# The matmuls of probabilities and values of a group, kept together and with the second head first

## The chip, the cores and the metric

The kernel runs on one core of a Trainium2 chip. The core has a matrix engine (TensorE, called PE; its weight loads are listed apart as PEld), VectorE (DVE), ScalarE (ACT), GpSimd (POOL) and SyncE (SP), which here issues the DMAs. Each engine works through its own queue in order and waits on semaphores for the others. TensorE writes to PSUM, in banks of 512 fp32 columns. The metric is the time of one execution on the device, in microseconds.

## The reference

Causal attention with a forget gate, over 4 batches, 8 heads, 576 positions and 64 values per head, and after it two feed-forward layers on the 2304 tokens:

```python
scores = scale * np.matmul(q, k.transpose(0, 1, 3, 2))
log_f = np.log(np.clip(f, 0.0001, 1.0))
cum = np.cumsum(log_f, axis=-1)
decay = cum[:, :, :, None] - cum[:, :, None, :]
scores = np.where(causal, -1000000000.0, scores + decay)
attn = np.exp(scores - np.max(scores, axis=-1, keepdims=True))
attn = attn / (np.sum(attn, axis=-1, keepdims=True) + 1e-09)
x = np.matmul(attn, v)                                  # then heads side by side: 2304 x 512
x = np.maximum(np.maximum(x @ w1, x @ w2), x @ w3) @ w_out          # d_ff 768
h = x @ w_in                                                        # d_ff 2048
P = a[0] + a[1] * h + a[2] * h*h + a[3] * h*h*h
Q = 1.0 + np.abs(b[0]) * np.abs(h) + np.abs(b[1]) * h*h
out = (P / (Q + 1e-06)) @ w_out2
```

## The kernel before, in words

Attention goes by pairs of heads, 20 pairs in all: the first batch has four pairs for the queries 0 to 319 (group 0) and again four for the queries 320 to 575 (group 1); each later batch has four pairs that do both groups. A unit is one head of a pair in one group; its names end in pair, head, group (`tp0_16_1_1` is of pair 16, head 1, group 1).

A unit goes through three steps of the outer loop (line 536). In its first step `scores` computes q times k into PSUM (L343, L345, L346), VectorE takes mask and row minimum (L347), ScalarE the exponential (L353), and `normalise` lets GpSimd scale the rows (L362). In the next step `turn` transposes the probabilities on TensorE, bank by bank (L382), and ScalarE copies them into `pt` (L384), which holds both heads of a group side by side. In the third step `attend` multiplies them with the values (L397), for both heads at once: it does nothing for head 0 and does the whole group when head 1 comes.

A group in `attend` has one PSUM bank `o`. Head 0 goes into partitions 0 to 63 and head 1 into 64 to 127 (`SIDES`). So each matmul has 64 columns of weights (the values of one head in one chunk of 128 keys), and the probabilities stream through. Group 0 has three key chunks, of 320, 256 and 128 queries; group 1 has five, four of 256 queries and one of 128. The program's order is chunk by chunk, and in each chunk head 0 and then head 1. These matmuls are plain fp32, and the trace has two records for each. A copy on ScalarE (L402) and a subtraction on VectorE (L403) then take the bank into the tile `x`, the input of the first feed-forward layer.

Between these pieces the loop puts, at six points of every step (`fill`), matmuls of the first feed-forward layer of finished batches: `moe1_h` (L427 to L429, tiles `h`) and `moe1_o` (L452 to L454, tiles `x2p`), and conversions of weights that are still to come. During the first four pairs, when there is no such work, `exercised` starts two matmuls without use (L84) ahead of each bank.

The engines' queues do not follow the program's order. All instructions up to line 762 are laid out by a scheduler with a timeline of its own: of the instructions whose inputs it takes as ready it picks by priority, normally the place in the program. `keep_in_program_order` (called by `pinned`, line 227) adds an edge from an instruction to the one traced just before it on the same engine, so that the two are not swapped; `tc.high_priority()` lets what is traced inside go first among the ready ones. After the attention comes the rest of the first layer with the conversion of the next weights (`raw_wi`, `convert_wi`), and then the second feed-forward layer, with an order written out by hand (line 763).

Of the kernel before, what the change touches and what calls it, by code (L numbers as in the profile page):

```python
# [37 lines left out]
def kernel(  # L38
    ctx: ExitStack, tc: tile.TileContext, q, k, v, f, w1, w2, w3, w_out, m2_in, m2_out, m2_a, m2_b, out
):  # L40
    nc = tc.nc
# [11 lines left out]
    def r32(ap):  # L53
        return ap.bitcast(F32)
# [25 lines left out]
    def exercised(bank, n):  # L80

        if n < 4:
            for _ in range(WARM):
                nc.tensor.matmul(bank, warm[:, 0], wide, start=True, stop=True)  # L84
        return bank
# [57 lines left out]
    for g in range(2):  # L143
        pts.append(apool.tile([P, 2, GCOLS[g]], F32, name=f"pt{g}", tag=f"pt{g}"))
        col = GCH[g][0][0]
# [81 lines left out]
    def pinned(ld):  # L227
        tc.keep_in_program_order(ld)
# [10 lines left out]
    SIDES = [(slice(0, D), slice(D, P)), (slice(D, P), slice(0, D))]  # L239
# [73 lines left out]
    class Unit:  # L313
# [72 lines left out]
        def attend(self):  # L386

            p, h, g = self.pair, self.h, self.g
            if h == 0:
                return  # L390
            lo, hi = GQ[g]
            w = hi - lo
            ot = exercised(ps_o.tile([P, 512], F32, name=f"o_{self.nm}", tag="o"), p.n)
            order = list(GCH[g].items())
            for j, (c, (col, q0)) in enumerate(order):
                for i in range(2):
                    nc.tensor.matmul(  # L397
                        ot[SIDES[i][0], q0 - lo : w], p.v[:, c, i], p.pt[g][:, i, col : col + hi - q0],
                        start=(j == 0), stop=(j == len(order) - 1),
                    )  # L400
            x = mpool.tile([P, 2, w], F32R, name=f"x_{self.nm}", tag=f"x{g}", bufs=(6, 8)[g])
            nc.scalar.activation(x[:, 0], ot[:, :w], AF.Copy)  # L402
            nc.vector.tensor_tensor(x[:, 1], ot[:, :w], r32(x[:, 0]), op=ALU.subtract)  # L403
            xt[p.b, p.hp, g] = x
# [390 lines left out]
```

## Time and profile before

| What | us |
| --- | --- |
| median of three timed runs | 983.41 (982.66 to 983.57) |
| span of the profiled execution, first to last instruction | 980.7 |
| PE busy, PEld busy | 962.0, 836.0 |
| VectorE, ScalarE, GpSimd busy | 742.8, 628.5, 254.1 |
| L397, matmuls of probabilities and values, 512 records | 78.5 |

The profiled execution has no time of its own beside its span; the 2.7 us between the span and the median lie before the first and behind the last instruction. Busy time of PE is the union of its records. Matmuls are pipelined, so records overlap: the time that one takes from the queue is read from its start to the next start, and not from its own length. L397 ends at about 496.5 us.

### The profile page before, as it was taken

To read this page: it belongs to the slowest core of one execution; us is meant where nothing else is said; L and a number is where in the kernel's file an instruction comes from. 1 tells how busy PE (TensorE), PEld (TensorE's weight loads), DVE (VectorE), ACT (ScalarE), POOL (GpSimd) and SP (SyncE) were. 2 spreads that over 40 slices of the span, in tenths; PEclk is the share of its full clock that TensorE was granted. 3 is DMA by queue.
4 is the path that set the end of the run, shared out by engine and by line. 5 is a ranking of instruction groups with operands and counts; after the bars stand their busy time and mean duration, and the time that the engine had idled before them with its cause. 6 is when DMAs were issued, how large, how long until landed. Compare 5 with 4: busy or idle time off the path is not lost.

```text
span 980.7 us, 16825 instructions
## 1 busy us (share of the span) xinstructions
PE 962.0 (98%) x5780; PEld 836.0 (85%) x5780; DVE 742.8 (76%) x1756; ACT 628.5 (64%) x1457; POOL 254.1 (26%) x408
## 2 busy tenths in 40 slices
PE   8989999999999999999999999999999999999998
PEld 6757898887889888999899987888888888899997
DVE  5789985556676777535367949988988888899997
ACT  5776666667666666646444538766666766677775
POOL 2555664445454545424223310000000000000000
PEclk9989999999999999999999999999999999999999
DMA  6594232124446455220054659011002100200000
GB/s 162 153 250 135 76 86 70 42 64 116 133 132 185 122 150 162 76 73 24 8 155 146 199 170 345 1 43 43 1 1 65 44 0 24 84 1 1 33 1 33
DMA packets 125621, 88.52 MB, mean 90 GB/s; under 512 B 74448, under 2 KB 110304, under 8 KB 125536
## 3 DMA queue, kind: packets, MB, share of 16 engines
q1 hardware_dynamic: 125536, 87.45, 29.8%
q8 instruction: 46, 0.75, 0.3%
q14 instruction: 39, 0.32, 0.1%
HBM read 64.73 MB, written 22.69 MB: 89 GB/s over the span
## 4 chain that ended last, share of the span: by engine, by line
PE 77%; DVE 6%; DMA 1%; issue 1%; ACT 1%; SPq 1%; POOL 0%; DVEq 0%; ACTq 0%
PE oo L718 7%; PE oo L719 7%; PE oo L717 7%; PE hq L668 6%; PE hq L670 6%; PE hq L669 6%; PE o L397 6%; PE h L427 5%; PE h L429 5%; PE h L428 5%; PE tp L382 4%; PE s L345 2%; PE s L346 2%; PE x2p L452 2%; PE x2p L454 2%; PE x2p L453 2%
## 5 line engine op out<-in xcount | busy, mean ns | idle before, releaser
L427 PE MATMUL h<-x,w1h 128*128 128x320 f32 (+1 forms) x576 | 177.1, 308 | 3.4 <-DVE m L434 3.0
L428 PE MATMUL h<-x,w1h 128*128 128x320 f32 (+1 forms) x576 | 172.3, 299 | 0.0
L429 PE MATMUL h<-x,w1l 128*128 128x320 f32 (+1 forms) x576 | 172.1, 299 | 0.0
L427 PEld LDWEIGHTS h<-x,w1h 128*128 128x128 f32 x576 | 109.6, 190 | 11.4 <-DVE m L434 5.2
L353 ACT ACTIVATE e<-e,st 128x64 f32<-128x64 f32 (+4 forms) x160 | 89.4, 559 | 46.0 <-DVE st L347 43.9
L362 POOL TENSOR_SCALAR e<-e,rs 128x64 f32<-128x64 f32 (+4 forms) x160 | 90.2, 578 | 105.5 <-DVE rs L359 80.9
L718 PE MATMUL oo<-wp,gh 128*128 128x512 f32 x288 | 112.8, 392 | 0.0
L717 PE MATMUL oo<-wp,gh 128*128 128x512 f32 x288 | 112.4, 390 | 0.0
L428 PEld LDWEIGHTS h<-x,w1h 128*128 128x128 f32 x576 | 109.8, 191 | 0.7 <-issue 0.6
L429 PEld LDWEIGHTS h<-x,w1l 128*128 128x128 f32 x576 | 109.6, 190 | 0.6 <-issue 0.6
L719 PE MATMUL oo<-wp,gl 128*128 128x512 f32 x288 | 108.8, 392 | 0.0
L677 ACT ACTIVATE s<-hq 128x512 f32<-128x512 f32 (+1 forms) x80 | 44.3, 554 | 96.9 <-PE hq L670 96.7
L347 DVE CUSTOM_DVE_ANT_0 e<-s,mask 128x320 f32<-128x320 f32 (+3 forms) x160 | 67.8, 433 | 49.2 <-PE s L346 34.6
L384 ACT ACTIVATE pt<-tp 128x384 f32<-128x384 f32 (+3 forms) x160 | 69.1, 470 | 19.6 <-PE tp L382 16.5
L680 DVE SCALAR_TENSOR_TENSOR s<-s,ab,u 128x512 f32<-128x512 f32 (+1 forms) x80 | 55.8, 698 | 31.3 <-ACT u L678 31.1
L382 PE MATMUL tp<-ident,e 128*128 128x128 f32 (+1 forms) x480 | 77.7, 282 | 0.9 <-POOL e L362 0.9
L397 PE MATMUL o<-pt,v 128*64 128x256 f32 (+2 forms) x512 | 78.5, 369 | 0.0
L670 PE MATMUL hq<-x,wil 128*128 128x512 f32 (+1 forms) x192 | 70.4, 366 | 0.0
L668 PE MATMUL hq<-x,wih 128*128 128x512 f32 (+1 forms) x192 | 70.4, 366 | 0.0
L669 PE MATMUL hq<-x,wih 128*128 128x512 f32 (+1 forms) x192 | 70.3, 366 | 0.0
L719 PEld LDWEIGHTS oo<-wp,gl 128*128 128x128 f32 x288 | 54.1, 188 | 11.7
L717 PEld LDWEIGHTS oo<-wp,gh 128*128 128x128 f32 x288 | 54.1, 188 | 11.0
(129 smaller groups left out, 2434.6 us busy)
## 6 DMA issues: line engine op xcount, KB each, us to landing
raw_w<-in_moe_w_dram SPq DMA_DIRECT2D x18, 512.0 KB
raw_wp<-in_moe_w_out_dram SPq DMA_DIRECT2D x32, 256.0 KB
wpd<-wp SPq DMA_DIRECT2D x32, 256.0 KB
raw_wi<-in_moe_w_in_dram SPq DMA_DIRECT2D x32, 256.0 KB
wp<-wpd SPq DMA_DIRECT2D x10, 768.0 KB
x2d<-xo SPq DMA_DIRECT2D x16, 320.0 KB
out_dram<-ob SPq DMA_DIRECT2D x18, 256.0 KB
kn<-in_k_dram SPq DMA_DIRECT2D x32, 128.0 KB
```

Source lines behind the costliest of these rows:

```text
L362: nc.gpsimd.tensor_scalar(e, e, self.rs[:, 1, j : j + 1], 0.0, op0=ALU.mult, op1=ALU.add)
L382: nc.tensor.transpose(tp[:kr, dst : dst + P], self.e[i][:, Q0[c] : Q1[c]], ident)
L397: nc.tensor.matmul(ot[SIDES[i][0], q0 - lo : w], p.v[:, c, i], p.pt[g][:, i, col : col + hi - q0], start=(j == 0), stop=(j == len(order) - 1),
L427: nc.tensor.matmul(hp_[:, :w], wh[:, j, dc], xs[dc][:, 1], start=(dc == NDC - 1), stop=False)
L428: nc.tensor.matmul(hp_[:, :w], wh[:, j, dc], xs[dc][:, 0], start=False, stop=False)
L429: nc.tensor.matmul(hp_[:, :w], wl[:, j, dc], xs[dc][:, 0], start=False, stop=(dc == 0))
L668: nc.tensor.matmul(hp_[:, :w], wih[:, dc, fs], xh, start=(dc == 0), stop=False)
L669: nc.tensor.matmul(hp_[:, :w], wih[:, dc, fs], xl, start=False, stop=False)
L670: nc.tensor.matmul(hp_[:, :w], wil[:, dc, fs], xh, start=False, stop=(dc == NDC - 1))
L717: nc.tensor.matmul(o, g[0][:, ts_], wh_, start=(fc == 0), stop=False)
L718: nc.tensor.matmul(o, g[0][:, ts_], wl_, start=False, stop=False)
L719: nc.tensor.matmul(o, g[1][:, ts_], wh_, start=False, stop=(fc == NF2 - 1))
```

## The change

In `attend` the loop over heads runs second head first. All matmuls of the group are traced at high priority, and each but the first is pinned to the one before it. The matmuls themselves, their operands and their bank are the same; the last `stop` of each half stays at the last chunk. Three lines are added, so that every line behind 400 has a number higher by three (L397 becomes L398, L427 becomes L430).

```diff
--- before.py
+++ after.py
@@ -392,12 +392,15 @@
             w = hi - lo
             ot = exercised(ps_o.tile([P, 512], F32, name=f"o_{self.nm}", tag="o"), p.n)
             order = list(GCH[g].items())
-            for j, (c, (col, q0)) in enumerate(order):
-                for i in range(2):
-                    nc.tensor.matmul(
-                        ot[SIDES[i][0], q0 - lo : w], p.v[:, c, i], p.pt[g][:, i, col : col + hi - q0],
-                        start=(j == 0), stop=(j == len(order) - 1),
-                    )
+            with tc.high_priority():
+                for j, (c, (col, q0)) in enumerate(order):
+                    for i in (1, 0):
+                        mm = nc.tensor.matmul(
+                            ot[SIDES[i][0], q0 - lo : w], p.v[:, c, i], p.pt[g][:, i, col : col + hi - q0],
+                            start=(j == 0), stop=(j == len(order) - 1),
+                        )
+                        if (j, i) != (0, 1):
+                            pinned(mm)
             x = mpool.tile([P, 2, w], F32R, name=f"x_{self.nm}", tag=f"x{g}", bufs=(6, 8)[g])
             nc.scalar.activation(x[:, 0], ot[:, :w], AF.Copy)
             nc.vector.tensor_tensor(x[:, 1], ot[:, :w], r32(x[:, 0]), op=ALU.subtract)
```

The queue of PE, group 1 of pair 16, before. Tiles `h` are the first feed-forward layer, `tp` transposes of probabilities, `s` scores. First the place at which the first matmul of the group stands:

```order
L427 MATMUL h1_2_0_3_5552<-x_12_1_0_3448,w1h_3_751 128x320
L428 MATMUL h1_2_0_3_5552<-x_12_1_0_3448,w1h_3_751 128x320
L429 MATMUL h1_2_0_3_5552<-x_12_1_0_3448,w1l_3_752 128x320
L397 MATMUL o_16_1_1_5572<-pt1_124,v_16_5029 64x256
L382 MATMUL tp0_16_1_1_5474<-ident_82,e3_16_1_1_5423 128x128
L382 MATMUL tp1_16_1_1_5498<-ident_82,e3_16_1_1_5423 128x128
L382 MATMUL tp2_16_1_1_5503<-ident_82,e3_16_1_1_5423 64x128
L345 MATMUL s0_0_17_1_0_5627<-k1s3_1339,q1s01_1627 128x64
```

and then, 44 rows further on, the place of the other nine:

```order
L382 MATMUL tp1_17_0_0_5619<-ident_82,e1_17_0_0_5515 64x128
L382 MATMUL tp1_17_0_0_5619<-ident_82,e2_17_0_0_5546 64x128
L429 MATMUL h0_2_0_4_5644<-x_12_1_0_3448,w1l_4_853 128x320
L397 MATMUL o_16_1_1_5572<-pt1_124,v_16_5029 64x256 x7
L397 MATMUL o_16_1_1_5572<-pt1_124,v_16_5029 64x128 x2
L427 MATMUL h1_2_0_4_5664<-x_15_1_0_4896,w1h_4_852 128x320
L428 MATMUL h1_2_0_4_5664<-x_15_1_0_4896,w1h_4_852 128x320
```

The same group after:

```order
L431 MATMUL h0_2_0_4_5644<-x_13_1_0_3914,w1h_4_852 128x320
L382 MATMUL tp0_17_0_0_5586<-ident_82,e1_17_0_0_5515 128x128
L382 MATMUL tp0_17_0_0_5586<-ident_82,e2_17_0_0_5546 128x128 x2
L382 MATMUL tp1_17_0_0_5619<-ident_82,e0_17_0_0_5509 64x128
L382 MATMUL tp1_17_0_0_5619<-ident_82,e1_17_0_0_5515 64x128
L398 MATMUL o_16_1_1_5572<-pt1_124,v_16_5029 64x256 x8
L398 MATMUL o_16_1_1_5572<-pt1_124,v_16_5029 64x128 x2
L382 MATMUL tp1_17_0_0_5619<-ident_82,e2_17_0_0_5546 64x128
L345 MATMUL s2_0_17_1_0_5639<-k1s3_1339,q1s01_1627 128x320
```

The lone matmul has joined the other nine, and they stand as one block: eight of 256 queries and two of 128.

In front of that block, after: the last transposes of the second head, from which its probabilities are copied. 28 rows stand between the last of them and the block, 20 of them `h`:

```order
L382 MATMUL tp0_16_1_1_5474<-ident_82,e4_16_1_1_5429 128x128
L382 MATMUL tp0_16_1_1_5474<-ident_82,e3_16_1_1_5423 128x128
L382 MATMUL tp0_16_1_1_5474<-ident_82,e4_16_1_1_5429 128x128
L382 MATMUL tp1_16_1_1_5498<-ident_82,e4_16_1_1_5429 128x128 x2
L382 MATMUL tp2_16_1_1_5503<-ident_82,e4_16_1_1_5429 64x128
L345 MATMUL s0_0_17_1_0_5627<-k1s3_1339,q1s01_1627 128x64
L430 MATMUL h2_2_0_3_5601<-x_15_1_0_4896,w1h_3_751 128x320
L431 MATMUL h2_2_0_3_5601<-x_15_1_0_4896,w1h_3_751 128x320
L432 MATMUL h2_2_0_3_5601<-x_15_1_0_4896,w1l_3_752 128x320
```

Before, 28 rows stood there too, in front of the nine matmuls, with a somewhat different mix.

The second place is early, group 1 of pair 4, the first group behind which first-layer work is there to fill. Before, seven matmuls stand behind the first two `h` tiles, and the other three further on:

```order
L429 MATMUL h1_0_0_0_911<-x_1_1_0_516,w1l_0_227 128x320
L427 MATMUL h1_0_0_0_911<-x_0_1_0_369,w1h_0_226 128x320
L428 MATMUL h1_0_0_0_911<-x_0_1_0_369,w1h_0_226 128x320
L429 MATMUL h1_0_0_0_911<-x_0_1_0_369,w1l_0_227 128x320
L397 MATMUL o_4_1_1_1028<-pt1_124,v_4_738 64x256 x7
L427 MATMUL h2_0_0_0_971<-x_3_1_0_841,w1h_0_226 128x320
L428 MATMUL h2_0_0_0_971<-x_3_1_0_841,w1h_0_226 128x320
```

After, all ten stand ahead of the first `h` tile, directly behind the transposes of pair 4 and one score matmul:

```order
L382 MATMUL tp1_4_1_1_962<-ident_82,e4_4_1_1_903 128x128 x2
L382 MATMUL tp2_4_1_1_967<-ident_82,e4_4_1_1_903 64x128
L343 MATMUL s4_1_5_1_1_1129<-kf3_113,qf3_117 128x256
L398 MATMUL o_4_1_1_1028<-pt1_124,v_4_738 64x256 x8
L398 MATMUL o_4_1_1_1028<-pt1_124,v_4_738 64x128 x2
L430 MATMUL h0_0_0_0_862<-x_3_1_0_841,w1h_0_226 128x320
L431 MATMUL h0_0_0_0_862<-x_3_1_0_841,w1h_0_226 128x320
L432 MATMUL h0_0_0_0_862<-x_3_1_0_841,w1l_0_227 128x320
L430 MATMUL h0_0_0_0_862<-x_2_1_0_661,w1h_0_226 128x320
```

Over the whole queue the 32 groups stand in 65 pieces before and in 32 after.

## Rows read from the trace of the kernel before

**Rows 1.** the page: span, busy time of the engines, chain that ended last

```profile
span 980.7 us, 16825 instructions
PE 962.0 (98%) x5780; PEld 836.0 (85%) x5780; DVE 742.8 (76%) x1756; ACT 628.5 (64%) x1457; POOL 254.1 (26%) x408
PE 77%; DVE 6%; DMA 1%; issue 1%; ACT 1%; SPq 1%; POOL 0%; DVEq 0%; ACTq 0%
```

**Rows 2.** windows: length, busy us (instructions) by engine, clock, DMA share, GB/s

```profile
0.00:62.00 62.00, 57.16 (x296) 42.85 (x297) 41.10 (x128) 43.26 (x118) 22.91 (x41) 1.00 0.67 181
62.00:120.00 58.00, 52.18 (x297) 43.09 (x296) 56.81 (x119) 36.40 (x85) 36.31 (x38) 0.85 0.45 127
120.00:500.00 380.00, 377.19 (x2809) 338.21 (x2809) 229.48 (x773) 236.00 (x671) 167.91 (x297) 1.00 0.35 98
500.00:981.00 481.00, 475.49 (x2383) 411.82 (x2381) 415.41 (x739) 312.85 (x585) 26.99 (x32) 1.00 0.20 68
```

**Rows 3.** PE's groups from 119 to 500 us: busy, mean ns, idle before

```profile
L345 PE MATMUL s<-k1s,q1s 128*128 128x448 f32 (+1 forms) x150 | 47.1, 321 | 1.3 <-DVE q1s L287 1.0 <-DVE st L347 0.4
L452 PE MATMUL x2p<-hh,wo 128*128 128x320 f32 (+1 forms) x144 | 43.9, 307 | 1.3 <-DVE xo L457 1.3
```

**Rows 4.** the chain around the last block of L397: start, us, what

```profile
494.40 2.10 PE o L397 x17
496.82 3.59 DMA raw_wi<-in_moe_w_in_dram
```

**Rows 5.** timeline of PE (start, us): rest of a split group, a whole group

```profile
27.08 1.40 PE L397 MATMUL o<-pt,v 128*64 128x320 f32 x10
...
351.56 1.41 PE L397 MATMUL o<-pt,v 128*64 128x320 f32 x12
```

**Rows 6.** timeline of PE: a lone matmul (two records) over 256 columns

```profile
92.32 0.31 PE L428 MATMUL h<-x,w1h 128*128 128x320 f32 x1
92.47 0.31 PE L429 MATMUL h<-x,w1l 128*128 128x320 f32 x1
92.71 0.65 PE L397 MATMUL o<-pt,v 128*64 128x256 f32 x2
93.28 0.41 PE L427 MATMUL h<-x,w1h 128*128 128x320 f32 x1
93.53 0.30 PE L428 MATMUL h<-x,w1h 128*128 128x320 f32 x1
```

**Rows 7.** timeline of PE: a lone matmul over 320 columns

```profile
57.60 0.75 PE L397 MATMUL o<-pt,v 128*64 128x320 f32 x2
58.28 0.48 PE L343 MATMUL s<-kf,qf 66*128 66x256 f32 x1
```

**Rows 8.** timeline of PE: the rest of a split group of ten

```profile
405.56 2.16 PE L397 MATMUL o<-pt,v 128*64 128x256 f32 x18
```

**Rows 9.** timeline: last transposes and last copy of that group's second head

```profile
400.86 0.82 PE L382 MATMUL tp<-ident,e 128*128 128x128 f32 x6
...
402.56 0.37 ACT L384 ACTIVATE pt<-tp 64x256 f32<-64x256 f32 x1
```

**Rows 10.** low clock: a wait of PE, a window, two h matmuls in it

```profile
65.09 0.90 PE L382 MATMUL tp<-ident,e 128*128 128x128 f32 x3 [0.65 <-POOL e L362]
...
66.00:78.00 12.00, 9.83 (x31) 7.16 (x32) 11.90 (x27) 8.06 (x18) 8.76 (x9) 0.50 0.55 158
...
77.17 0.47 PE L427 MATMUL h<-x,w1h 128*128 128x320 f32 x1
77.44 0.47 PE L428 MATMUL h<-x,w1h 128*128 128x320 f32 x1
```

**Rows 11.** windows of L397 alone: length, PE, PEld, clock, DMA, GB/s

```profile
20.00:62.00 42.00, 8.62 (x48) 4.33 (x48) 1.00 0.76 211
62.00:120.00 58.00, 6.24 (x42) 3.23 (x42) 0.85 0.45 127
120.00:500.00 380.00, 63.68 (x423) 33.00 (x422) 1.00 0.35 98
```

## Prediction

> **What bounds the kernel now.** I read the page's busy shares and its chain first, then a table of windows by stage, then TensorE's waits, and last the changed line, L397, piece by piece in the timeline. The span is 980.7 us; with the 2.7 us that lie around it in the timed runs this is the median of 983.4 us, and I work every sum against that. PE is named busy for 98% of the span and holds 77% of the chain that ended last [rows 1]. By stage [rows 2]: up to 62 us the pipeline fills; from 62 to 120 us VectorE is busy 56.8 of 58 us and PE runs partly at a low granted clock; from 120 to 500 us PE is busy 377 of 380 us while VectorE and ScalarE are at about 60%; after 500 us the last feed-forward work runs, without any L397. In the long stretch PE waits for almost nothing: 1.3 us before the scores and 1.3 us before x2p are its only waits of a microsecond or more [rows 3]. So between 120 and 500 us the time is the sum of what PE has to start, one matmul after the other, and anything taken out of that queue comes off the end.
>
> What follows 500 us moves along rather than absorbing it: the chain goes from the last block of L397 at 494.40 straight to the first load of raw_wi at 496.82 [rows 4], and the conversions that fill the next stage hang on that load.
>
> **The change, part by part.** L397 writes two heads into two halves of one bank: each matmul uses 64 of the 128 columns of the array. Two such matmuls of different heads run side by side. The one whole group in the trace shows it: its six matmuls last 1.41 us, and the rest of a split group, with one matmul less, lasts 1.40 us [rows 5]. The first matmul of the first head, when it stands next to its partner, is free.
>
> Before, it mostly does not stand there. The first head's probabilities are ready a step earlier, so the scheduler put its first matmul alone into some other work, and the remaining nine or five matmuls later. A group of the first kind is 320 queries by three key chunks (six matmuls), one of the second 256 queries by five (ten). In the order, the 32 groups are in 65 pieces: 14 groups of the first kind have their first matmul apart, and so have 15 of the second, whose 16th (pair 4) is broken further in; three of the first kind have a break (or one more) before the last chunk; only one stands whole. After, the 32 groups are 32 pieces, all with heads alternating.
>
> What a lone matmul costs, over 256 columns [rows 6]: it starts at 92.71 and the next starts at 93.28, so 0.57 us. The matmul in front of it takes 0.24 us to the next start instead of the 0.15 us of its neighbour: 0.09 us. The one behind takes 0.25 us instead of 0.15: 0.10 us. Sum 0.76 us. Over 320 columns [rows 7]: 0.68 us from start to start, and with the same 0.19 us of entry and exit 0.87 us.
>
> What the rest costs does not grow when the lone one returns: for the first kind of group it is seen (1.40 against 1.41 us). For the second kind no whole group is in the trace. The rest of a split one lasts 2.16 us for 18 records [rows 8]; the second head has all five of its chunks in there and the first head only four, so the second head's column half sets the length and the fifth chunk lies beside it. Bounds: 2.16 us if that holds, 2.16 + 0.57 us if not. I take 2.16, since the smaller group behaves so.
>
> The sum of PE time removed: 16 groups of the second kind x 0.76 = 12.2 us; 14 of the first kind x 0.87 = 12.2 us; three further breaks at 0.2 us (entry and exit alone) = 0.6 us. Together 25.0 us. By stage: four lone matmuls before 62 us, 3.5 us; two groups between 62 and 120 us, 1.5 us; the rest, 20.0 us, in the stretch where PE is the bound.
>
> Of the 5.0 us before 120 us I take half, 2.5 us: the bounds are 0 (VectorE, 56.8 of 58 us busy, sets the pace there [rows 2]) and 5.0 (up to 62 us PE is busy for 57.2 us [rows 2], and VectorE's work would start earlier too).
>
> **What the change adds** is one wait per group: the whole block now stands behind the second head's copy of the probabilities, and PE issues in order, so all behind it would stand too: the transposes of the next unit, whose copies ScalarE would get late, and the h matmuls. In the trace, for the group of pair 16, the last transposes start at 400.86 and end at 401.68, and the last copy starts at 402.56 and takes 0.37 us, so it lands at 402.93; the block starts at 405.56 [rows 8, 9]. The copy needs 1.3 us behind the transposes. In the new order 28 rows stand between these transposes and the block: 20 h matmuls at 0.15 us [rows 6], four score matmuls and five transposes, about 3.8 us (an estimate from these durations). Ahead of nearly all blocks the new order keeps such a distance, a little shorter than before; only pair 4's block stands close behind its transposes, in the stretch that PE does not bound. So I price new waits at the size of the existing ones: 0 at best, 2.6 us (a doubling of the two waits of [rows 3]) at worst, taken at 1.3 us. Bringing the rest of the program into another order costs nothing by itself: the count of h, score and transpose matmuls is the same, and a change between transposes and full matmuls is paid before and after alike.
>
> ScalarE, VectorE, GpSimd and the queues get the same instructions. Their loads move by a few places only, and the DMA share of 0.35 from 120 to 500 us leaves room for all of it to come 5% sooner [rows 2].
>
> Forecast: 983.4 - 20.0 - 2.5 + 1.3 = 962.2, so **962 us**. Its own range: with all 25.0 us and no new wait 958.4, with the two present waits gone too 955.8; with nothing gained before 120 us and all new waits 966; I let it reach 969.
>
> **Rivals.** [...]
>
> *PE is not the bound, and the time goes into waits.* Weight loads fill 338.2 of the 380 us only [rows 2], so 41.8 us are left, more than the 20 us removed; were those waits in disguise, the block would merely wait longer elsewhere and the time stay at 983. Against it: L397 itself holds the weight loads for only 33.0 of its 63.7 us [rows 11], which explains 30.7 of the 41.8. [...]
>
> *Slower: the copy is late at every block.* If PE reached each block when the second head's last transposes are just done, it would stand for the 1.3 us worked out from [rows 9] at each of 32 blocks, 41 us, against 25 us removed: 983 + 16 = 999. It decides where less than about 0.5 us of other PE work stands between (1.3 less the 0.8 us that a group gains). The order has this at one block of 32.
>
> *The heads do not pair as written,* since each chunk now starts with the second head. Then only entry and exit are saved, 33 x 0.19 = 6 us: 977. The 1.41 us of the whole group [rows 5] speak against: alternation is what pairs, and which head leads should not matter.
>
> **How the numbers follow.** Forecast 0.74 (956 to 969); early stretch or new waits eat a part 0.11 (969 to 979), the pairing rival with it 0.03; better than computed 0.03; no change 0.04; slower 0.05. The range 955 to 976 holds the first and about half of the second. A measurement of this kernel tells about 0.2%, 2 us, from no change: faster 0.91, within 0.04, slower 0.05.
>
> **What would show it.** In the new trace the attention line should be in 32 pieces of 1.41 and 2.16 us, 57 us busy in sum against 78.5 now [rows 11]; the last block should start near 473 us against 494.40 [rows 4]; the time from there to the end should be as now. PE's waits should not show a new one of more than 1 us on ScalarE's copy in front of the block. I would be wrong if the last block starts less than 12 us earlier, if a whole group of the second kind lasts over 2.3 us, or if the part after the last block is longer than before.

## The result: 15 us faster, and the profile after

| | before | after |
| --- | --- | --- |
| median of the timed runs, us | 983.49 (982.66 to 983.73) | 968.42 (966.44 to 970.9, 4 runs) |
| span of the profiled execution, us | 980.7 | 969.1 |

The ratio is 0.9849, with a 95% interval of 0.9837 to 0.9861: 15 us faster. The prediction was 962 us, in a range of 955 to 976. The profiled execution of the changed kernel took 970.9 us, the longest of its four, so the two traces are only 11.6 us apart. On record each execution takes 1.8 us more than its span (970.9 against 969.1); the 2.7 us that I put around the span before hold, beside these, 0.9 us by which that execution was shorter than the median. I work sums against the traces and keep verdicts to the medians.

The page after, answering to [rows 1], and the table of cores, whose last number is the mean granted clock:

```profile
span 969.1 us, 16846 instructions
...
PE 943.1 (97%) x5780; PEld 829.9 (86%) x5780; DVE 739.6 (76%) x1756; ACT 623.8 (64%) x1457; POOL 252.4 (26%) x408
...
PE 70%; DVE 14%; DMA 6%; ACT 4%; issue 3%; POOL 2%; SPq 1%; ACTq 0%; POOLq 0%; DVEq 0%
```

```profile
core 0: 969.1 us, clock 0.988
```

PE's busy time fell by 18.9 us, from 962.0 to 943.1, but the span by 11.6 only. What is not busy rose from 18.7 (980.7 less 962.0) to 26.0 us. VectorE now holds 14% of the chain that ended last, where it held 6%. The windows, answering to [rows 2]:

```profile
0.00:62.00 62.00, 54.79 (x300) 41.42 (x300) 41.24 (x134) 44.15 (x122) 23.87 (x42) 1.00 0.69 183
62.00:120.00 58.00, 51.61 (x299) 42.80 (x299) 54.13 (x113) 35.36 (x86) 37.28 (x40) 0.85 0.43 123
120.00:500.00 380.00, 373.72 (x2890) 346.32 (x2889) 240.89 (x805) 239.10 (x684) 169.90 (x301) 0.99 0.37 103
...
120.00:160.00 40.00, 37.59 (x255) 34.06 (x254) 27.29 (x87) 24.75 (x69) 17.80 (x31) 0.91 0.34 93
160.00:485.00 325.00, 321.13 (x2531) 297.27 (x2530) 200.21 (x683) 206.82 (x596) 147.58 (x264) 1.00 0.37 103
```

Up to 62 us PE does 2.4 us less than in [rows 2] in the same 62 us: the work was taken out, and PE stood still instead. From 120 to 160 us it is idle for 2.4 us, at a clock of 0.91. From 160 us on it is nearly full again. PE's timeline shows the blocks, answering to [rows 5, 8] (the last row is the last block of all, answering to [rows 4]):

```profile
341.17 0.28 PE L430 MATMUL h<-x,w1h 128*128 128x256 f32 x1
341.38 1.41 PE L398 MATMUL o<-pt,v 128*64 128x320 f32 x12
342.72 0.39 PE L431 MATMUL h<-x,w1h 128*128 128x256 f32 x1
...
396.27 2.17 PE L398 MATMUL o<-pt,v 128*64 128x256 f32 x20
...
481.35 2.17 PE L398 MATMUL o<-pt,v 128*64 128x256 f32 x20
```

They are as forecast: 12 records in 1.41 us, 20 in 2.17 us, 32 pieces. From start to start all 512 records take 56.9 us, against 74.0 before. But the last block starts 13 us earlier, at 481.35, and not 21 us. PE's waits say where part of it went (engine, line and tile that waits, what for: us in sum, times, the longest):

```profile
PE h L430 <- ACT m L435: 2.2, 2, 1.2
PE x2p L456 <- POOL wo L179: 2.0, 1, 2.0
PE x2p L455 <- DVE xo L460: 1.9, 1, 1.9
PE x2p L455 <- ACT hh L441: 1.6, 2, 1.3
PE s L345 <- DVE q1s L287: 1.5, 1, 1.5
PE s L343 <- ACT qf L283: 0.9, 1, 0.9
PE o L398 <- DVE x L406: 0.8, 1, 0.8
...
PE o L398 <- ACT pt L384: 0.4, 1, 0.4
```

Only the last row is the wait that I named as the danger, the block on ScalarE's copy, and it is 0.4 us at one block. Not all of the others are new. Before, the waits of `h` and `x2p` had these rows among the longest:

```profile
PE h L427 <- DVE m L434: 3.0, 3, 2.0
...
PE x2p L452 <- DVE xo L457: 1.3, 1, 1.3
...
PE x2p L452 <- ACT hh L438: 0.6, 2, 0.3
```

Summed by the tile that waits, `x2p` went from 1.9 to 5.7 us, the block `o` itself from 0 to 1.3, and the transposes `tq` and `tk` from 4.8 to 6.7, while `h` fell from 3.4 to 2.8 and `s` stayed at 3.0. So what grew most are waits of `x2p` for conversions and elementwise work. The longest of them, in the timeline, and two windows:

```profile
138.05 0.54 PE L455 MATMUL x2p<-hh,wo 128*128 128x320 f32 x2
140.61 0.41 PE L456 MATMUL x2p<-hh,wo 128*128 128x320 f32 x1 [2.02 <-POOL wo L179]
...
144.14 0.47 PE L455 MATMUL x2p<-hh,wo 128*128 128x320 f32 x1
144.41 0.47 PE L456 MATMUL x2p<-hh,wo 128*128 128x320 f32 x1
```

```profile
62.00:79.00 17.00, 15.23 (x52) 9.43 (x52) 15.74 (x36) 10.93 (x26) 11.58 (x12) 0.52 0.59 159
141.00:148.00 7.00, 6.86 (x28) 6.33 (x27) 3.57 (x11) 3.32 (x10) 3.63 (x9) 0.51 0.48 142
```

PE reaches the last w_out tile before GpSimd has made it, stands for 2.02 us, and then runs for 7 us at a granted clock of 0.51: an x2p matmul takes 0.27 us from start to start there, and 0.15 from 148.0 us on, at 1.00.

### The profile page after: what moved, and what is told of

It reads as the page before. It is cut to its first block, busy times and chain, and to the rows that moved or that the text cites. A ratio compares the mean times of both kernels' runs of the same rounds, so it can differ in the third digit from the quotient of the medians.

```text
span 969.1 us, 16846 instructions
## 1 busy us (share of the span) xinstructions
PE 943.1 (97%) x5780; PEld 829.9 (86%) x5780; DVE 739.6 (76%) x1756; ACT 623.8 (64%) x1457; POOL 252.4 (26%) x408
## 4 chain that ended last, share of the span: by engine, by line
PE 70%; DVE 14%; DMA 6%; ACT 4%; issue 3%; POOL 2%; SPq 1%; ACTq 0%; POOLq 0%; DVEq 0%
PE oo L721 7%; PE oo L722 7%; PE oo L720 7%; PE hq L671 6%; PE hq L673 6%; PE hq L672 6%; PE tp L382 4%; PE h L430 4%; PE o L398 4%; PE h L431 4%; PE h L432 4%; PE x2p L455 2%; DMA raw_wi<-in_moe_w_in_dram 2%; PE x2p L456 2%; PE x2p L457 2%
## 5 line engine op out<-in xcount | busy, mean ns | idle before, releaser
L430 PE MATMUL h<-x,w1h 128*128 128x320 f32 (+1 forms) x576 | 176.6, 307 | 3.1 <-ACT m L435 2.2
L430 PEld LDWEIGHTS h<-x,w1h 128*128 128x128 f32 x576 | 109.4, 190 | 7.0 <-ACT m L435 3.0
L362 POOL TENSOR_SCALAR e<-e,rs 128x64 f32<-128x64 f32 (+4 forms) x160 | 87.7, 563 | 106.4 <-DVE rs L359 91.5
L722 PEld LDWEIGHTS oo<-wp,gl 128*128 128x128 f32 x288 | 54.1, 188 | 11.7
L720 PEld LDWEIGHTS oo<-wp,gh 128*128 128x128 f32 x288 | 54.2, 188 | 11.0
L721 PEld LDWEIGHTS oo<-wp,gh 128*128 128x128 f32 x288 | 54.1, 188 | 10.9
```

The lines of the kernel that those rows point to most:

```text
L362: nc.gpsimd.tensor_scalar(e, e, self.rs[:, 1, j : j + 1], 0.0, op0=ALU.mult, op1=ALU.add)
L430: nc.tensor.matmul(hp_[:, :w], wh[:, j, dc], xs[dc][:, 1], start=(dc == NDC - 1), stop=False)
L720: nc.tensor.matmul(o, g[0][:, ts_], wh_, start=(fc == 0), stop=False)
L721: nc.tensor.matmul(o, g[0][:, ts_], wl_, start=False, stop=False)
L722: nc.tensor.matmul(o, g[1][:, ts_], wh_, start=False, stop=(fc == NF2 - 1))
```

## An account that all kernels can be put into

For each kernel I split the span into three terms. **Idle** is the span less PE's busy time. **Clock** is the span times one less the mean granted clock. That is an estimate which takes PE's pace as proportional to this clock; at about half clock the changed kernel's trace has 0.56 of the pace for the x2p matmuls above (0.15 against 0.27 us) and 0.52 for a block of ten (2.10 us against 4.04). **Work** is the rest, PE's queue at full clock. "Pieces" is in how many pieces the 32 groups stand in PE's queue.

| kernel | pieces | median | span | idle | clock | work |
| --- | --- | --- | --- | --- | --- | --- |
| before | 65 | 983.5 | 980.7 | 18.7 | 8.8 | 953.2 |
| after | 32 | 968.4 | 969.1 | 26.0 | 11.6 | 931.5 |
| after, run again | 32 | 967.8 | 969.6 | 28.3 | 8.7 | 932.6 |
| e1, first head first | 64 | 989.6 | 987.0 | 25.6 | 3.0 | 958.4 |
| e7, head order alone | 36 | 975.6 | 975.8 | 30.3 | 8.8 | 936.7 |
| e4, head by head | 32 | 992.6 | 992.8 | 23.7 | 8.9 | 960.2 |
| e5, from pair 8 | 40 | 967.5 | 965.8 | 21.2 | 6.8 | 937.8 |
| e6, up to pair 7 | 57 | 989.6 | 989.2 | 26.6 | 12.9 | 949.7 |
| e9, conversions at 0.6 | 32 | 970.1 | 968.6 | 28.3 | 10.7 | 929.6 |
| e9, conversions at 0.7 | 32 | 975.2 | 973.3 | 30.1 | 11.7 | 931.5 |
| e10, e6 with 0.6 | 57 | 986.5 | 985.9 | 28.1 | 9.9 | 947.9 |
| e11, before with 0.6 | 66 | 994.5 | 990.6 | 24.2 | 9.9 | 956.5 |
| e12, lighter VectorE | 32 | 958.0 | 955.8 | 21.7 | 0 | 934.1 |
| e13, before, lighter VectorE | 66 | 982.1 | 979.9 | 19.0 | 6.9 | 954.0 |

Leaving e4 aside, which changes what a block costs, the work follows the pieces: 930 to 934 us at 32, 937 and 938 at 36 and 40, 948 and 950 at 57, 953 to 958 at 64 to 66. That is about 0.7 us for each piece. Idle and clock follow no such rule; between kernels idle differs by up to 12 us and clock by up to 13. The split has limits: the mean clock has three digits, which is half a microsecond, and a wait that lies inside a stretch of low clock is counted in both terms, by 3 us at most (e9 with 0.6).

Idle and clock also differ between executions of one kernel: the changed kernel run again has 2.3 us more idle time and 2.9 us less clock loss than in its first profile. The mean clock is on record for most timed executions. In eight of the changed kernel it is 0.988 to 0.993, a loss of 10.2 us on average, and in 36 of the kernel before 0.991 to 0.997, a loss of 6.3 us.

## The experiments

In the expectations A is the prediction's theory; the other letters are rivals, as each text says, and D and E of the fourth experiment are new ones. The kernel before was run beside each group of runs, with medians of 983.0 to 984.4 us; the ratios are to those.

**1. Which part of the edit joins the pieces.** The pins by themselves were not run, so no run here shows what they do alone. Two kernels were run: pins and priority with the old order of heads (e1),

```diff
-                    for i in (1, 0):
+                    for i in (0, 1):
...
-                        if (j, i) != (0, 1):
+                        if (j, i) != (0, 0):
```

> Pins and high priority as in the change, only the heads go in the old order: first head, then second, in each chunk. In PE's order the first matmul of every group then stands alone again: 64 pieces. Theory A (the gain is PE time of lone matmuls that now run beside their partner, with what a lone one costs at entry and exit): the gain is gone, 981 to 986 us, and lone pieces of 0.57 and 0.68 us are back. Rival C (the gain comes from the high priority, which lays the whole program out differently): 966 to 972 us, as with the change.

and the kernel before with the order of heads alone (e7).

```diff
-                for i in range(2):
+                for i in (1, 0):
```

> The kernel before with one edit: in each chunk the second head goes first; no pins, no high priority. PE's order has 36 pieces, the four extra breaks behind an even number of matmuls or in the middle of group 0. Theory A: nearly the whole gain, 967 to 973 us. Rival C: little or none of it, 978 to 984 us.

e1 took 989.63 us (988.78 to 990.07), ratio 1.0053 (1.0038 to 1.0068): 6 us slower than before, outside both expectations. Its timeline has the lone matmuls back, as [rows 6, 8] have them:

```profile
401.62 0.31 PE L432 MATMUL h<-x,w1l 128*128 128x320 f32 x1
401.86 0.65 PE L398 MATMUL o<-pt,v 128*64 128x256 f32 x2
402.43 0.41 PE L430 MATMUL h<-x,w1h 128*128 128x320 f32 x1
...
410.56 2.16 PE L398 MATMUL o<-pt,v 128*64 128x256 f32 x18
```

High priority and pins without the new head order win nothing. By the account e1 has 6.9 us more idle time and 5.2 us more work than before and 5.8 us less clock loss; why its queue is longer at 64 pieces than the one before at 65 was not looked into. e7 took 975.57 us (974.38 to 977.58), ratio 0.9913 (0.9895 to 0.9932), between the two expectations. Its work is 16.5 us below before, so the head order by itself takes most of the queue time. The 7 us that it lacks against the changed kernel are 4.3 us more idle time and 5.2 us more work, less 2.8 us of clock. So the head order is what joins: the first matmul of a group now needs the second head's probabilities and can't go ahead alone. Priority and pins together take away the last four breaks; the 4.3 us of idle time are a difference of single profiles.

**2. One block, heads not alternating** (e4).

```diff
-                for j, (c, (col, q0)) in enumerate(order):
-                    for i in (1, 0):
+                for i in (1, 0):
+                    for j, (c, (col, q0)) in enumerate(order):
```

> The change with its loops swapped: all chunks of the second head, then all of the first, pinned and at high priority. 32 pieces as with the change, with the same entries and exits, but heads do not alternate. Theory A: a block lasts the sum of its two heads, 3.9 us instead of 2.1 for group 1 and about 2.5 instead of 1.34 for group 0; 16 x 1.8 + 16 x 1.2 = 48 us more, where PE is the bound: 1008 to 1017 us. Rival B (what counts is that the block stands in one piece, with fewer entries and exits): 966 to 972 us.

It took 992.6 us (992.33 to 994.57), ratio 1.0083 (1.0067 to 1.01), 24 us over the changed kernel. In its timeline the same blocks last longer:

```profile
407.96 3.51 PE L398 MATMUL o<-pt,v 128*64 128x256 f32 x20
411.40 0.55 PE L382 MATMUL tp<-ident,e 128*128 128x128 f32 x3
...
423.88 2.00 PE L398 MATMUL o<-pt,v 128*64 128x320 f32 x12
425.81 0.55 PE L297 MATMUL tq<-ident,qn 128*128 128x128 f32 x3
```

3.44 us from start to next start instead of 2.10, and 1.93 instead of 1.34, in one unbroken piece in both. So the pairing is in the alternation of the heads. The expected size was too large: at the hand-over from one head to the other some matmuls still ran side by side. In the block at 407.96 us the first head's records begin at 409.31 us, and the second head's last one begins at 409.84 us.

**3. Halves.** The change for pairs 8 to 19 alone (e5) and for pairs 0 to 7 alone (e6), with the changed kernel run again beside them:

```diff
+            if p.n >= 8:        # e6: p.n < 8
                 with tc.high_priority():
...
+            else:
+                for j, (c, (col, q0)) in enumerate(order):
+                    for i in range(2):
...
```

> The change for pairs 8 to 19 alone; pairs 0 to 7, the first batch (about the first 150 us), keep the old loop. Theory A with the early stretch giving its part back (in the trace of the change the copy behind the block of pair 7 comes 3.7 us later than before, and all the gain lies behind it): 963 to 967 us, faster than the change. Rival D (the early gain is real and the loss is elsewhere): the 5 us of the first six lone matmuls and pair 7's are missing, 971 to 975 us.

> The change for pairs 0 to 7 alone, the rest as before. Theory A with the early stretch giving back: 982 to 987 us, no gain or a small loss. Rival D: 977 to 980 us.

> The change itself, unaltered, timed again beside the two halves: 966 to 971 us by its four runs so far. If the two halves add up, its distance to the kernel before is the sum of theirs.

e5 took 967.48 us (966.87 to 969.94), ratio 0.984 (0.9823 to 0.9857); e6 989.58 (988.47 to 990.94), ratio 1.006 (1.0047 to 1.0074); the changed kernel again 967.8, ratio 0.9847 (0.9827 to 0.9866). The later pairs alone give all of the gain. The early pairs alone take 3.5 us out of the queue and cost 6 us: e6 has 7.9 us more idle time than before and 4.1 us more clock loss. The halves sum to -9.4 us and the whole is -15.4, so idle and clock of a half are not those that it has within the whole.

**4. Is it the wait for w_out?** The changed kernel, e6 and before, with the weights converted earlier in the program (0.7 in a further run of the changed kernel):

```diff
-        state["c"] += 0.15 if step < 7 else 0.5
+        state["c"] += 0.15 if step < 7 else 0.6
```

> The changed kernel with one number different: from step 7 on, weight conversions are traced at 0.6 instead of 0.5 per call of fill, so those of w_out come earlier in the program. Theory D (the early stretch loses what it saves, because PE waits 2.02 us for the last w_out conversions at 138.6 us and then runs 6.9 us at half clock): without that wait the low clock at 141 to 148 us goes too, 2.0 + 3.5 = about 5.5 us less, 961 to 964. Theory E (the early stretch gives nothing because VectorE sets its pace; wait and low clock are only where it shows): same as the changed kernel, 966 to 970, with another wait in place of this one. The scheduler moves the x2p matmuls forward along with the conversions, so the wait may stay under another tile; then D is not tested and the trace says so.

> As the run with 0.6, with 0.7 conversions per call. Theory D: 960 to 964 if the wait in front of x2p is gone. Theory E: 966 to 970. If faster conversions crowd VectorE earlier, between 90 and 120 us, slower than the changed kernel: 970 to 974.

> The change for pairs 0 to 7 alone (989.6 us, with the same 2 us wait and low clock from 141.8 to 148.6), and conversions at 0.6. Theory D: 982 to 985, level with the kernel before. Theory E: 988 to 991.

> The control: the kernel before, without the change, with conversions at 0.6. It has neither the 2 us wait on w_out nor the low clock at 141 to 148 us, so by theory D nothing is to be won: 982 to 985. By theory E, with VectorE setting the pace, 982 to 985 too. A gain of over 3 us here would mean that the number helps by itself, whatever the change does.

The changed kernel took 970.1 us with 0.6, ratio 0.9866 (0.9852 to 0.9881), and 975.22 with 0.7, ratio 0.992 (0.9903 to 0.9936). e10 took 986.5, ratio 1.0033 (1.002 to 1.0046). The control e11, which should have stayed where it was, took 994.53, ratio 1.0113 (1.0097 to 1.0129). Of the changed kernel with 0.6, two windows, and one row of PE's timeline:

```profile
64.00:84.00 20.00, 13.81 (x48) 8.40 (x48) 16.27 (x36) 11.32 (x26) 13.74 (x12) 0.50 0.61 179
141.00:148.00 7.00, 6.76 (x50) 6.51 (x50) 3.66 (x10) 4.24 (x12) 4.72 (x10) 1.00 0.46 139
```

```profile
77.46 0.90 PE L382 MATMUL tp<-ident,e 128*128 128x128 f32 x3 [4.15 <-POOL e L362]
```

The 2 us wait and the low clock at 141 us are gone, together, and the time is not won. Another wait, of 4.15 us, stands at 77 us, and the early low clock reaches to 84 us. Theory D (that wait is the loss) falls for the changed kernel; E had another wait in its place, and 970 us at most. With 0.7 it is slower than either theory gave, on the side of the crowded VectorE. In e10 the number wins 3 us, half of what D gave it; in e11 it costs 11 us, which neither theory had: in the profile it is 9.9 us, 5.5 of idle time, 3.3 of work and 1.1 of clock, among them 7 us of low clock behind a wait of 1.61 us at 366 us. It is no way to a faster kernel.

**5. Less work for VectorE before 140 us.** The clamp is left out of the conversion of the first layer's weights, in the changed kernel (e12) and in the one before (e13):

```diff
-        nc.vector.tensor_scalar(tf, tf, E_LO, E_HI, op0=ALU.max, op1=ALU.min)
+        if not nm_.startswith(('w0', 'w1', 'w2', 'wo')):
+            nc.vector.tensor_scalar(tf, tf, E_LO, E_HI, op0=ALU.max, op1=ALU.min)
```

> The changed kernel, with VectorE given less to do before 140 us: the clamp of exponents in the conversion of the first layer's weights (L170, 30 instructions, 14.1 us of VectorE in the kernel before between 20 and 140 us) is left out. Theory E (VectorE sets the pace up to 150 us, so what the change takes from PE there is not seen): with VectorE lighter the time falls by 5 to 10 us against the changed kernel, to 958 to 963. Theory D' (the early loss is bad luck of the schedule, waits and low clock that come with any new order of instructions): the time may go either way, 964 to 972.

> The kernel before, with the same clamp left out of the same 30 conversions. The question is the distance to the changed kernel with the clamp out. Theory E: PE sets the pace earlier, so the change saves up to 3.7 us more than the 15.4 us of the full kernels: 973 to 979 here, and the changed one 18 to 20 us below. Theory D': the distance moves by as much as the new order of instructions happens to give, in either direction, 5 us or so around 16.

e12 took 958.01 us (957.23 to 959.83), ratio 0.9738 (0.9722 to 0.9755); e13 982.05 (981.08 to 984.36), ratio 0.998 (0.997 to 0.9991). The same 30 instructions of VectorE, 14 us in the kernel before, are worth 10 us to the changed kernel and some 2 us to the one before (984.4 us in these runs), and the change by itself is worth 24.0 us between these two. e12's page, cores, a window that holds the early low clock of the others, and its last block:

```profile
span 955.8 us, 16814 instructions
...
PE 934.1 (98%) x5780; PEld 823.1 (86%) x5780; DVE 729.2 (76%) x1726; ACT 625.8 (65%) x1457; POOL 250.7 (26%) x408
```

```profile
core 0: 955.8 us, clock 1.000
```

```profile
62.00:80.00 18.00, 15.35 (x101) 11.51 (x102) 16.64 (x36) 13.91 (x32) 13.53 (x11) 1.00 0.75 210
```

```profile
469.37 2.17 PE L399 MATMUL o<-pt,v 128*64 128x256 f32 x20
```

and the same window of e13:

```profile
62.00:80.00 18.00, 13.39 (x45) 9.20 (x43) 17.73 (x33) 11.12 (x25) 12.31 (x12) 0.62 0.78 216
```

Between e13 and e12 the work is 19.9 us less, the idle time 2.7 us more and the clock loss 6.9 us less: 24.1 us. In e12 PE starts 101 instructions in these 18 us, in e13 45. Theory E was right in direction and on e12's time, but not on e13's, for which it gave 973 to 979 us; the distance came out 4 us larger than E gave and 3 us larger than D' gave. The clock, which E did not speak of, is most of e12's gain on the changed kernel: its four executions lose 1.0 us to it on average, the eight of the changed kernel 10.2 us, and 10 us is what e12 is faster. So E's own mechanism, VectorE setting the pace, is not shown by its time. That the clock holds nearly throughout is seen in this one kernel of those run (1.000 in three of its four executions), so I don't claim that it follows from the lighter VectorE alone. e12 is the fastest kernel of the study, but one without the clamp; of the full ones the changed kernel and e5 are level.

## Why the prediction was right, and where 6 us went

The measured 968.4 us lies at the upper edge of the 956 to 969 us that had the chance of 0.74. The worst sum that I had worked out was 966 us; the rest up to 969 was an allowance with no term behind it, and it was needed. The mechanism held from 155 us on, and the early stretch went the other way.

**PE's queue is the bound from 120 to 500 us: right.** From the eighth group's copy into `x` (at 155 us after) to the 32nd the changed kernel gains 16.6 us on the one before; with 0.6 it gains 15.9 us over that stretch and e12 15.6. The two copies, before and then after, in ScalarE's timeline:

```profile
151.34 0.39 ACT L402 ACTIVATE x<-o 128x256 fp32r<-128x256 f32 x1 [1.02 <-PE o L397]
...
496.53 0.39 ACT L402 ACTIVATE x<-o 128x256 fp32r<-128x256 f32 x1 [1.71 <-PE o L397]
```

```profile
154.99 0.38 ACT L405 ACTIVATE x<-o 128x256 fp32r<-128x256 f32 x1 [0.91 <-PE o L398]
...
483.56 0.38 ACT L405 ACTIVATE x<-o 128x256 fp32r<-128x256 f32 x1 [4.54 <-PE o L398]
```

The work follows the number of pieces, in twelve kernels (all but e4). The 41.8 us that the weight loads left free were no sign against the gain: they are busy for 346.3 of the 380 us now, against 338.2 [rows 2], and the queue's time was taken out all the same.

**25.0 us of PE time removed: right in kind, somewhat too large.** The account has 21.7 us, 20.6 with the changed kernel run again, and 19.9 between e13 and e12. The lone matmuls themselves were priced rightly: 16 at 0.57 and 14 at 0.68 us are 18.6 us, and L397's records take 17.1 us less from start to start (18.3 between e13 and e12), though pair 4's block now stands at a clock of 0.50 and takes 4.04 instead of 2.10 us. Entry and exit, 33 x 0.19 = 6.3 us, are the mis-sized term: some 1.6 to 2.7 us are left for them (19.9 less 18.3 between e13 and e12; 21.7 less the 19.0 that L397's records would take less with pair 4 at full clock). I had read them from a lone matmul between h matmuls; of the 29 lone ones of before only four have h or x2p matmuls on both sides. That this is the reason was not tested.

**A whole group of ten at 2.16 us: right** (2.17, and 2.10 to the next start). So was that only one block would stand close behind its copy.

**2.5 us gained before 120 us: wrong; the early stretch lost time.** By the rows above the changed kernel is 3.7 us late at the eighth copy (3.9 us when run again), gains 16.6 us up to the 32nd, and is 1.4 us longer behind it: 3.7 - 16.6 + 1.4 is -11.5, the -11.6 us seen but for rounding. That is worse than the lower of my two bounds, which was 0. The windows up to that copy, before and then after:

```profile
0.00:151.34 151.34, 140.16 (x809) 113.61 (x810) 122.49 (x322) 101.32 (x264) 77.44 (x109) 0.94 0.53 144
```

```profile
0.00:155.00 155.00, 138.99 (x811) 113.39 (x812) 121.00 (x326) 100.98 (x266) 78.01 (x110) 0.92 0.51 139
```

PE's idle time there grew by 4.8 us, from 11.2 to 16.0, and low clock took 3.5 us more (an estimate: half of the 7.0 us by which 24.0 us at a clock of 0.50 to 0.51 exceed 17.0 us at 0.50, the stretches listed below), so that the 4.6 us by which its queue got shorter were more than given back. Changing the early pairs alone (e6) makes that copy 4.0 us late, leaving them (e5) 0.5 us. Up to 62 us the 2.4 us taken from PE became 2.4 us of idle time.

**New waits 1.3 us: wrong, 7.3 us.** I had priced only the waits that the new blocks could make. What came were waits elsewhere. By the windows, PE's idle time grew by 2.4 us up to 62 us, by 0.6 to 120 us, by 3.5 to 500 us and by 0.9 behind that. PE reaches conversions and elementwise results sooner, and not all of these come sooner: the waits of `x2p` alone grew by 3.7 us, those of the blocks by 1.3.

**The clock, taken as unchanged: 2.8 us lost in these two traces.** The early low stretch became a little longer (62.5 to 79.6 us, against 64.7 to 78.3), a new one lies at 141.0 to 147.9, and one at 98.8 to 102.2 went. (The fall at 64.7 us lies inside the wait of [rows 10], which ends at 65.1.) No run shows a term behind the 969 to 979 us that had the chance of 0.11 (early stretch or new waits); the eight executions of the changed kernel took 966.44 to 971.38 us. In the run again the stretches are others (69.1 to 79.3, 96.4 to 99.8 and 144.2 to 147.6 us), and the loss is that of the kernel before; over all executions on record it is about 4 us more.

**The part after the last block: nearly as forecast.** It takes 487.7 us against 486.3, and 489.4 in the run again; by my own sign of being wrong, a longer part, this is a small miss. In the other kernels it takes 485.7 to 490.4 us. By the traces, -21.7 + 7.3 + 2.8 is the -11.6 us seen, and with the run again -20.6 + 9.6 - 0.1 is -11.1; forecast was -21.2. So the sum of the lost idle time and clock is firm, and its division is not. The medians differ by 3.5 us more than the traces.

What stays open: why one schedule meets these waits and low clocks and another does not. Experiment 4 shows that taking away one of them brings another. The rivals "no pairing", "PE not the bound" and "the copy is late at every block" are out, by e4's and the changed kernel's blocks, by the account, and by the waits.

## What to carry to other kernels

Matmuls that use half of the array's columns paid here only as neighbours (a block of ten took 2.10 us with the heads alternating and 3.44 us head by head): look in the queue's order, not in the program's, for a first one that its data lets go ahead alone, and make it depend on what its partner needs. Time taken from the bounding queue did not come off the end in full here (21.7 us of work less, 11.6 us of span), with waits for its feeders and low clock in its place; add up queue, idle time and clock for before and after separately, since each moved here by several microseconds. And where an engine sets the pace in an early stretch, relieving another one there may win nothing until the first is lighter; e12, with 14 us less on VectorE and 10 us below the changed kernel, fits this and does not prove it, since most of its gain is clock.

## What the runs showed of the hardware

The granted clock fell to about half behind some waits of PE and not behind others of much the same length. In the changed kernel it fell to 0.51 behind 2.02 us at 140.6 us, while 1.88 us at 354.2 us left it at 1.00. In e7 it fell to 0.50 at 294.2 us, at the end of the shorter of these two waits, and not behind the longer (timeline, then windows):

```profile
294.53 0.64 PE L452 MATMUL x2p<-hh,wo 128*128 128x320 f32 x1 [1.45 <-DVE xo L457]
...
527.33 0.41 PE L452 MATMUL x2p<-hh,wo 128*128 128x320 f32 x1 [2.23 <-ACT hh L438]
```

```profile
294.20:297.60 3.40, 3.07 (x11) 3.07 (x12) 0.83 (x6) 1.62 (x6) 2.06 (x3) 0.50 0.59 190
527.30:530.70 3.40, 3.37 (x23) 3.38 (x24) 1.38 (x3) 1.17 (x3) 0.74 (x1) 1.00 0.13 44
```

The stretches at 141.0 us here and at 366 us in e11, both at 0.51, stand directly behind a wait, of 2.02 and 1.61 us; the rows of e7 show that the length of the wait alone does not tell whether the clock falls: it fell behind 1.45 us and not behind 2.23. The changed kernel run again has the first of these waits too, 2.03 us at 141.6 us, and then 3.4 us of low clock instead of 6.9.

In the first profile the 7 us of low clock cost about 3.5 us (an estimate: 7 us at a clock of 0.51), more than the 2 us wait in front of them. And in e4, where all matmuls of one head precede those of the other, a block of ten took 3.44 us instead of the 3.9 us expected: I had not expected that some would still run side by side there.
